# Decode attention over two head blocks: the load order of the last units, finer pieces of the last K and V, and the place of two unit sums on the matmul engine

## The chip, the cores and the metric

The kernel runs on one core of one Trainium2 chip. The metric is the device time of one execution in microseconds (us). Lower is better. The kernel before takes 1973.36 us, the median of 3 runs (1972.6 to 1973.85).

## What is computed

The reference is one decode step of attention for two independent blocks, A and B, of the same shape, whose outputs stand side by side. Each block has a batch of 2, one query token, 32 heads, 8192 cached positions and a head width of 192, all in bf16:

```python
q = (x @ wq).reshape(B, Sq, Hq, Dh).transpose(0, 2, 1, 3)       # x: 2 x 1 x 640
scores = einsum("bhqd,bhkd->bhqk", q, k_cache) * (Dh ** -0.5)   # 8192 scores a head
p = softmax(scores, axis=-1)
o = einsum("bhqk,bhkd->bhqd", p, v_cache)
out = o.transpose(0, 2, 1, 3).reshape(B, Sq, Hq * Dh) @ wo      # 2 x 1 x 640
```

Every element of both caches is used once. The caches are nearly all of the 836.77 MB that the kernel reads.

## The kernel before

**Units.** The work is cut into 64 units, numbered 0 to 63. Unit u is one pair of heads (hp = u // 2, 32 pairs over both blocks) for one batch element (b = u % 2). Its K is one transfer of 6144 KB, and its V another. Both go to one of three buffers `kv` of 128 partitions, in which each of the two heads has 64 partitions, and each partition has T = 128 positions of 192 values.

**The steps of a unit.** Times are those of the profile.

- VectorE (DVE) multiplies K by the broadcast query, in four chunks of 32 positions: `dve_mul`, L226, 3.35 us each, into two `prod` buffers in turn. A chunk needs the sums of the chunk two before it to be done, since they read the same buffer.
- TensorE (PE) adds up a chunk's products: `pe_sum`, L309, 12 matmuls against the identity. For most units the four chunks stand in a loop of instructions (`pe_sums`); for units 62 and 63 they stand one by one.
- DVE finishes the sums (`dve_red`, L229) and takes the maximum (`dve_max`, L235). GpSimd (POOL) brings the maximum to all partitions (L218). ScalarE (ACT) makes the exponentials (`act_nb` L251, `act_exp` L259), and POOL and DVE the sum's reciprocal (L221, L243).
- PE multiplies by V: `pe_pv`, L329, 64 matmuls for one unit. It is called the V product below.
- For each pair of heads, ACT takes the result out of PSUM (`act_f1`, L268), PE turns it (`pe_f3`, L339, 12 matmuls for a pair, or 6 for one batch element), ACT scales it (`act_f4`, L275), and PE multiplies it by `wo` (`pe_f5`, L352, 6 matmuls).

**The order of each engine** is written out by hand. Each step is put in a table at a slot (about the unit) with an order number inside the slot, and the engine runs its table in that order. What an engine is told to wait for blocks all that stands behind it. In most slots u, PE runs the sums of unit u, the `f3` of a finished pair and then the V product of unit u - 1. At the end the order of PE is another one: the sums of units 62 and 63 are in slot 61 (L376, order 1.9), so PE runs the sums of 61, 62 and 63, and only then the V products of 60, 61 and 62. The V product of 63 is cut in pieces that follow its loads, with the `f3` of batch element 0 after the first. The last four `f5` (pairs 28 to 31) close the program.

**Loads.** All K, V and `wo` loads are issued by SyncE (SP), in one queue and in the order of the list `loads` (L138 to L146). Load number i goes to buffer i % 3, and SP waits before it until load i - 3 is used up: `done()`, L431, which is the last `dve_mul` for a K and the last V product matmul for a V. The list alternates: K of unit u, then V of unit u - 1. At the end, lines 144 to 146 take K 62 and K 63 out and put them ahead of V 60. So the last loads are K 61, K 62, K 63, V 60, V 61, V 62, V 63. `VSPLIT` cuts V 62 in two halves and V 63 in pieces of 1/2, 1/4, 1/8, 1/16 and 1/16, and each piece has a semaphore of its own. `KSPLIT` is empty. The four parts of the last `wo` follow V 63 (L448), and each of the last four `f5` waits for its part.

Of the kernel before, what the change touches and what calls it, by code (L numbers as in the profile page):

```python
# [58 lines left out]
def build_kernel(nc, blocks, out):  # L59
# [4 lines left out]
    T = Sk // 64  # L64
# [8 lines left out]
    PW = HW // 2  # L73
    UW = PW * B
    NW = NBLK * Hn // HW
    NP = NBLK * Hn // 2
    NU = NP * B
    LASTP = NP - 1
    LASTU = NU - 1
# [8 lines left out]
    with ExitStack() as es:  # L88
# [35 lines left out]
        S_sp = _Stream("sp", sem("s_sp"), reg)  # L124
# [6 lines left out]
        xsem = [sem(f"xsem{k}") for k in range(NBLK)]  # L131
        osem = [sem(f"osem{k}") for k in range(NBLK)]

        KSPLIT = {}
        VSPLIT = {LASTU - 1: [0, T // 2, T],
                  LASTU: [0, T // 2, 3 * T // 4, 7 * T // 8, 15 * T // 16, T]}

        loads = []  # L138
        for u in range(NU):
# [1 line left out]
            if u >= 1:  # L141
                loads.append(("v", u - 1))
        loads.append(("v", LASTU))
        for u in (LASTU - 1, LASTU):
            loads.remove(("k", u))
            loads.insert(loads.index(("v", LASTU - 3)), ("k", u))  # L146
        buf = {}
        bcount = [0] * NBUF
        for i, (kind, u) in enumerate(loads):
# [29 lines left out]
        def back(name, u, c, n):  # L179
            i = u * NCH + c - n  # L180
            return (name, i // NCH, i % NCH) if i >= 0 else None
# [124 lines left out]
        def pe_sum(c):  # L306
            def fn(eng):
                for j in range(NJ):
                    ins = eng.matmul(scps[c % 2][:], ident[:], prod[c % 2][:, :, j * DG:(j + 1) * DG],  # L309
                                     start=(j == 0), stop=(j == NJ - 1))  # L310
                return ins
            return fn
# [21 lines left out]
        def pe_f3(bs):  # L334
            def fn(eng):
                for b in bs:
                    for i in range(3):
                        for s in range(2):
                            ins = eng.matmul(oTps[64 * s:64 * s + 64, 2 * i + b:2 * i + b + 1],  # L339
                                             o_sb[:, b, :].rearrange("p (r i) -> p i r", i=3)[:, i, :],  # L340
                                             sel[:, s:s + 1], start=True, stop=True)
                return ins
            return fn

        def pe_f5(hp):
            first = (hp % PPB == 0)
            last = (hp % PPB == PPB - 1)

            def fn(eng):
                for i in range(3):  # L350
                    for half in range(2):
                        ins = eng.matmul(outps[0:4, 0:NH2], oTz[:, hp % NZ, i, 2 - 2 * half:6 - 2 * half],  # L352
                                         wo_t[:, hp % PW, i, half * NH2:(half + 1) * NH2],
                                         start=(first and i == 0 and half == 0),
                                         stop=(last and i == 2 and half == 1))
                return ins
            return fn
# [4 lines left out]
        pe_tab = [[] for _ in range(NSLOT)]  # L362
        pool_tab = [[] for _ in range(NSLOT)]

        def put(tab, slot, order, fn, waits, sig):
            tab[slot].append((order, len(tab[slot]), fn, waits, sig))

        for u in range(NU):
            hp = u // B
            for c in range(NCH):  # L370
                kw = [("k", u, c)] if u in KSPLIT else [("k", u)]
                put(dve_tab, u, 2 + 2 * c, dve_mul(u, c), kw + [("a0", u), back("s", u, c, 2)], ("m", u, c))
                put(dve_tab, u, 2 + 2 * min(c + 1, NCH - 1) + 1, dve_red(u, c),
                    [("s", u, c), key("mx", u - 2), key("exp", u - 2)], ("r", u, c))
                if u >= LASTU - 1:
                    put(pe_tab, LASTU - 2, 1.9, pe_sum(c), [("m", u, c), back("r", u, c, 2), ("init",)], ("s", u, c))  # L376
            if u < LASTU - 1:
                put(pe_tab, u, 0, pe_sums(u), [back("r", u, 1, 2), ("init",)], [("s", u, c) for c in range(NCH)])
            put(dve_tab, u, 12, dve_max(u), [("r", u, NCH - 1), key("ar", u - 2), ("init",)], ("mx", u))
            put(pool_tab, u, 0, pool_ar(u), [("mx", u), key("nb", u - 2)], ("ar", u))  # L380
            put(pool_tab, u, 1, pool_ls(u), [("exp", u), key("f2", u - 2)], ("ls", u))
            put(dve_tab, u + 1, 14, dve_f2(u), [("ls", u), key("f4", hp - 2)], ("f2", u))
            put(act_tab, u, 0, act_nb(u), [("ar", u), key("exp", u - 2)], ("nb", u))
            put(act_tab, u, 1, act_exp(u), [("nb", u), key("pv", u - 2), key("ls", u - 2), ("init",)], ("exp", u))
            w0 = [("exp", u), key("f1", hp - 2), ("init",)]
            cuts = VSPLIT.get(u)
            if cuts is None:
                put(pe_tab, u + 1, 2, pe_pv(u, 0, TJ), w0 + [("v", u)], ("pv", u))
            else:
                for i, (t0, t1) in enumerate(zip(cuts[:-1], cuts[1:])):  # L390
                    put(pe_tab, u + 1, 2 + 0.01 * i, pe_pv(u, t0 // 2, t1 // 2), (w0 if i == 0 else []) + [("v", u, i)],
                        ("pv", u) if t1 == T else None)
            sl = UW * (u // UW - 1) + 5 + (u % UW) // 2 if u >= UW else (u - 1) // 2
            order = (-1 if u < 2 else 4)
            put(pe_tab, max(sl, 0), order, pe_q(u), [("wq", u // UW), ("xbc", hp // PPB)], ("pq", u))
            put(act_tab, max(sl, 0), order, act_a0(u), [("pq", u), back("m", u - NQ, NCH - 1, 0)], ("a0", u))

        for hp in range(NP):
            u0, u1 = 2 * hp, 2 * hp + 1
            w1 = [key("f3", hp - 1), ("init",)]  # L400
            w3 = [("sel",), ("init",)]
            w4 = [("f2", u0), key("f5", hp - NZ), ("init",)]
            if hp < LASTP:
                put(act_tab, u1 + 1, 2, act_f1(hp, 0, 2), [("pv", u0), ("pv", u1)] + w1, ("f1", hp))
                put(pe_tab, u1 + 2, 1.5 if hp < LASTP - 1 else 2.5, pe_f3((0, 1)), [("f1", hp)] + w3, ("f3", hp))
                put(act_tab, u1 + 2, 3, act_f4(hp, (0, 1)), [("f3", hp), ("f2", u1)] + w4, ("f4", hp))
            else:
                put(act_tab, u1 + 1, 2, act_f1(hp, 0, 1), [("pv", u0)] + w1, ("f1a", hp))
                put(pe_tab, u1 + 1, 2.005, pe_f3((0,)), [("f1a", hp)] + w3, ("f3a", hp))
                put(act_tab, u1 + 1, 3, act_f4(hp, (0,)), [("f3a", hp)] + w4, ("f4a", hp))  # L410
                put(act_tab, u1 + 2, 2, act_f1(hp, 1, 2), [("pv", u1), ("f3a", hp)], ("f1", hp))
                put(pe_tab, u1 + 2, 1.5, pe_f3((1,)), [("f1", hp)] + w3, ("f3", hp))
                put(act_tab, u1 + 2, 3, act_f4(hp, (1,)), [("f3", hp), ("f2", u1), ("f4a", hp)], ("f4", hp))
            w = hp // PW
            w5 = [("f4", hp), key("f5", hp - 1)]
            if hp % PPB == 0 and hp > 0:
                w5.append(("oev", hp // PPB - 1))
            if w < NW - 1:
                sl = UW * w + 11
                put(pe_tab, sl, 1.6, pe_f5(hp), w5 + [("wo", w)], ("f5", hp))  # L420
            else:
                sl = NU + 1
                put(pe_tab, sl, 1.4 if hp % PW == 0 else 1.6, pe_f5(hp), w5 + [("wol", hp % PW)], ("f5", hp))
            if hp % PPB == PPB - 1:
                blk = hp // PPB
                put(act_tab, sl, 5, act_out(blk), [("f5", hp)], ("oev", blk))
                put(act_tab, sl, 6, out_dma(blk, 0), [("oev", blk)], None)
                if blk < NBLK - 1:
                    put(act_tab, sl, 7, out_dma(blk, 1), [("oev", blk)], None)
# [6 lines left out]

        S_sp.add(sp_wq(0))
        for i, (kind, u) in enumerate(loads):
            for n, fn in enumerate(sp_kv(kind, u)):
                S_sp.add(fn, waits=[done(i - NBUF)] if n == 0 else [])  # L440
            if kind == "k":
                if u % UW == 5 and u // UW + 1 < NW:
                    w = u // UW
                    S_sp.add(sp_wq(w + 1), waits=[("pq", UW * w + UW - 1), key("f5", PW * w - 1)])
                if u >= UW + 3 and u % UW == 3:
                    w = u // UW - 1
                    S_sp.add(sp_wo(w), waits=[("pq", UW * (w + 1) + UW - 1)])
        for q in range(PW):  # L448
            S_sp.add(sp_wo(NW - 1, q), waits=[("f5", PW * (NW - 1) - 1)])
        S_sp.add(out_dma(NBLK - 1, 1), waits=[("oev", NBLK - 1)])  # L450

        S_pool.add(lambda eng: eng.memset(ident[:], 1.0), sig=("id0",))
# [108 lines left out]
```

## Time and profile before

| what | value |
|---|---|
| median of the runs shown | 1973.36 us (1972.6 to 1973.85, 3 runs) |
| the profiled execution: device time | 1973.09 us |
| the profiled execution: span on the core | 1971.4 us |
| granted clock of TensorE, mean | 0.956 |
| PE busy | 1571.2 us (80%) |
| DVE busy | 1067.4 us (54%) |
| ACT, POOL busy | 196.5 us, 60.2 us |
| read from HBM | 836.77 MB, 424 GB/s over the span |
| rate from 100 to 1700 us | 431 GB/s, DMA busy share 1.00 |

The span is 1.69 us shorter than the device time of the same execution. Times inside the program are given from the start of the span. The time between a load's issue and its landing is read from the table of DMA issues, asked for a window around the issue; a landing is the issue plus that time. "x64" in a row is the number of instructions merged in it, and a bracket at its end is the idle time before it and what ended it.

### The profile page before, as it was taken

What the parts mean: (1) busy time and instruction counts of PE and PEld (TensorE: products, weight loads), DVE (VectorE), ACT (ScalarE), POOL (GpSimd) and SP (SyncE); (2) the same over time, 40 slices, a digit from 0 to 9 for tenths busy, and PEclk for the clock granted to TensorE, in tenths of its full rate; (3) what the DMA queues carried; (4) which work ended last, traced back from release to release, by engine and by line L of the source; (5) the groups of instructions that cost most, each with busy time, mean ns of one, the idle gap of its engine ahead of it and who ended that gap; (6) DMA issues with size and microseconds to landing.
All of it is one profiled execution on the core that took longest, in us unless ns stands there. A gap on an engine that the chain in (4) does not pass through costs nothing.

```text
span 1971.4 us, 19404 instructions
## 1 busy us (share of the span) xinstructions
PE 1571.2 (80%) x8448; PEld 772.2 (39%) x8448; DVE 1067.4 (54%) x772; ACT 196.5 (10%) x647; POOL 60.2 (3%) x145
## 2 busy tenths in 40 slices
PE   3887877878778688787887878877788777888769
PEld 1443434434334344343443434433344333443325
DVE  5664565545654556545556455464554654645570
ACT  0110110001100011000110101100011001110001
POOL 1000000000000000000000000000000000000000
PEclk9998999989989899998999989999999999999989
DMA  9999999999999999999999999999999999999986
GB/s 403 431 431 434 431 431 434 430 426 434 431 432 427 435 434 430 429 426 435 433 433 427 431 434 431 431 427 434 430 430 433 432 427 433 435 433 425 434 374 272
DMA packets 29334, 837.81 MB, mean 425 GB/s; under 512 B 3016, under 2 KB 3024, under 8 KB 12624
## 3 DMA queue, kind: packets, MB, share of 16 engines
q1 hardware_dynamic: 28676, 836.77, 98.9%
q8 instruction: 55, 0.90, 0.2%
q10 hardware_dynamic: 588, 0.01, 0.0%
q14 instruction: 15, 0.12, 0.0%
HBM read 836.77 MB, written 0.01 MB: 424 GB/s over the span
## 4 chain that ended last, share of the span: by engine, by line
DMA 50%; PE 28%; DVE 19%; issue 2%; ACT 0%; SPq 0%
DMA kv<-in_A_k_cache_dram 24%; DMA kv<-in_B_k_cache_dram 24%; PE ops L329 18%; DVE prod L226 17%; PE scps L309 9%; DVE sc L229 2%; DMA kv<-in_B_v_cache_dram 2%; PE outps L352 0%; PE qps L339 0%; PE qps L301 0%; DVE mp L235 0%; SPq L185 0%; ACT qbc L284 0%; DVE rcT L243 0%; ACT out_sb L289 0%
## 5 line engine op out<-in xcount | busy, mean ns | idle before, releaser
L226 DVE TENSOR_TENSOR prod<-kv,qbc 128x6144 bf16<-128x6144 bf16 x256 | 852.7, 3351 | 637.7 <-DMA kv<-in_B_k_cache_dram 321.0
L309 PE MATMUL scps<-prod,ident 128*128 128x512 bf16 x3072 | 769.5, 407 | 360.3 <-DVE prod L226 360.3
L329 PE MATMUL ops<-kv,pb 128*34 128x384 bf16 x4096 | 676.6, 326 | 1.3 <-DMA kv<-in_B_v_cache_dram 1.1
L309 PEld LDWEIGHTS scps<-prod,ident 128*128 128x128 bf16 x3072 | 300.2, 103 | 822.2 <-DVE prod L226 459.1
L329 PEld LDWEIGHTS ops<-kv,pb 128*34 128x34 bf16 x4096 | 395.6, 98 | 274.1 <-issue 15.5
L229 DVE TENSOR_REDUCE sc<-scps 128x32 f32<-128x512 f32 x256 | 175.8, 687 | 201.8 <-PE scps L309 201.8
L251 ACT ACTIVATE nb<-mg 64x1 f32<-64x1 f32 x128 | 25.7, 201 | 1313.6 <-POOL mg L218 1312.8
L301 PE MATMUL qps<-wbuf,xbc 128*128 128x384 bf16 x320 | 64.7, 334 | 35.0 <-ACT qbc L284 24.5
L259 ACT ACTIVATE pb<-sc,nb 64x128 bf16<-64x128 f32 x128 | 81.7, 638 | 31.9 <-PE ops L329 28.8
L218 POOL PARTITION_ALL_REDUCE mg<-mp x64 | 26.0, 406 | 1716.5 <-DVE mp L235 1716.5
L284 ACT ACTIVATE qbc<-qps 64x192 bf16<-64x192 f32 x128 | 41.6, 325 | 181.5 <-PE qps L301 180.3
L301 PEld LDWEIGHTS qps<-wbuf,xbc 128*128 128x128 bf16 x320 | 26.5, 99 | 70.3 <-ACT qbc L284 36.8
L268 ACT ACTIVATE o_sb<-ops 2x384 f32<-2x384 f32 (+1 forms) x66 | 31.1, 471 | 223.9 <-PE ops L329 223.5
L339 PEld LDWEIGHTS qps<-sel,o_sb 34*64 34x64 f32 x768 | 36.3, 171 | 13.6 <-issue 13.3
L339 PE MATMUL qps<-sel,o_sb 34*64 34x1 f32 x768 | 39.1, 225 | 0.0
L259 ACT ACTIVATION_READ_ACCUMULATOR pb<-sc,nb 64x1 f32 x128 | 38.6, 301 | 0.0
L235 DVE TENSOR_REDUCE mp<-sc 64x1 f32<-64x128 f32 x128 | 35.9, 280 | 3.1
L243 DVE RECIPROCAL rcT<-lall 64x1 f32<-64x1 f32 x128 | 20.1, 157 | 25.4 <-POOL lall L221 22.5
L221 POOL PARTITION_ALL_REDUCE lall<-rs x64 | 27.9, 436 | 157.5 <-ACT pb L259 157.5
L352 PE MATMUL outps<-wbuf,oTz 128*4 128x320 bf16 x192 | 31.3, 299 | 1.4
L352 PEld LDWEIGHTS outps<-wbuf,oTz 128*4 128x4 bf16 x192 | 13.7, 84 | 16.3 <-PE outps L352 8.9
L275 ACT ACTIVATE oTz<-qps,rcT 128x3 bf16<-128x3 f32 x64 | 13.7, 268 | 15.5 <-PE qps L339 14.7
(19 smaller groups left out, 15.8 us busy)
## 6 DMA issues: line engine op xcount, KB each, us to landing
kv<-in_A_k_cache_dram SPq DMA_DIRECT2D x32, 6144.0 KB, 29.6
kv<-in_A_v_cache_dram SPq DMA_DIRECT2D x32, 6144.0 KB, 29.4
kv<-in_B_k_cache_dram SPq DMA_DIRECT2D x32, 6144.0 KB, 30.3
kv<-in_B_v_cache_dram SPq DMA_DIRECT2D x30, 6144.0 KB, 30.4
kv<-in_B_v_cache_dram SPq DMA_DIRECT2D x3, 3072.0 KB, 12.0
wbuf<-in_A_wq_dram SPq DMA_DIRECT2D x4, 1920.0 KB, 33.1
wbuf<-in_A_wo_dram SPq DMA_DIRECT2D x4, 1920.0 KB, 32.5
wbuf<-in_B_wq_dram SPq DMA_DIRECT2D x4, 1920.0 KB, 33.5
```

The source lines that it names most:

```text
L221: return lambda eng: eng.partition_all_reduce(lall[u % 2][:], rs[u % 2][:], 128, bass.bass_isa.ReduceOp.add)
L226: return lambda eng: eng.tensor_tensor(prod[c % 2][:], t[:, c * TC:(c + 1) * TC, :], q, ALU.mult)
L229: return lambda eng: eng.tensor_reduce(sc[u % 2][:, c * TC:(c + 1) * TC], scps[c % 2][:], AXL.X, ALU.add)
L235: ins = eng.tensor_reduce(mp[u % 2][r, s:s + 1], sc[u % 2][r, :], AXL.X, ALU.max)
L259: ins = eng.activation(pb[u % 2][r, :, s::32], sc[u % 2][r, :].rearrange("p (j a) -> p j a", a=2), ACTF.Exp, bias=nb[u % 2][r, :], scale=s ...
L268: ins = eng.activation(o_sb[r, b0:b1, :], ops[hp % 2][r, b0:b1, a * Dh:(a + 1) * Dh], ACTF.Identity)
L284: ins = eng.activation(qbc[u % NQ][r, :], qps[r, s * Dh:(s + 1) * Dh], ACTF.Identity)
L301: ins = eng.matmul(qps[:, 0:QW], xbc[b][:, c, :], wq_t[:, c, off:off + QW], start=(c == 0), stop=(c == DC - 1))
L309: ins = eng.matmul(scps[c % 2][:], ident[:], prod[c % 2][:, :, j * DG:(j + 1) * DG], start=(j == 0), stop=(j == NJ - 1))
L329: ins = eng.matmul(ops[(u // B) % 2][0:MP, u % B, 0:QW], pb[u % 2][:, j, :], vv[:, j, :], start=(j == 0), stop=(j == TJ - 1))
L339: ins = eng.matmul(oTps[64 * s:64 * s + 64, 2 * i + b:2 * i + b + 1], o_sb[:, b, :].rearrange("p (r i) -> p i r", i=3)[:, i, :], sel[:, s: ...
L352: ins = eng.matmul(outps[0:4, 0:NH2], oTz[:, hp % NZ, i, 2 - 2 * half:6 - 2 * half], wo_t[:, hp % PW, i, half * NH2:(half + 1) * NH2], sta ...
```

## The change

- The special order of the last K loads is removed. K and V alternate to the end: K 61, V 60, K 62, V 61, K 63, V 62, V 63.
- K 62 and K 63 are loaded in four quarters each, one for each chunk of the multiply, with a semaphore for each. V 61 is now in halves as V 62 is, and V 63 is in seven pieces: 1/4, 1/4, 1/8, 1/8, 1/8, 1/16 and 1/16.
- On PE the sums of 62 and 63 stand in their own slots. The order becomes: sums 61, `f3` of pair 29, V product 60, sums 62, V product 61, sums 63, `f3` of pair 30, V product 62, V product 63 in seven pieces.
- The `f5` of pair 28 is moved ahead of the last three pieces of the V product of 63, and its part of `wo` ahead of V 63 in the queue of SP.

No arithmetic is added or removed. From K 62 on, the K and V loads go from 10 transfers to 19.

```diff
-        KSPLIT = {}
-        VSPLIT = {LASTU - 1: [0, T // 2, T],
-                  LASTU: [0, T // 2, 3 * T // 4, 7 * T // 8, 15 * T // 16, T]}
+        QUART = [0, T // 4, T // 2, 3 * T // 4, T]
+        HALF = [0, T // 2, T]
+        KSPLIT = {LASTU - 1: QUART, LASTU: QUART}
+        VSPLIT = {LASTU - 2: HALF, LASTU - 1: HALF,
+                  LASTU: [0, T // 4, T // 2, 5 * T // 8, 3 * T // 4, 7 * T // 8, 15 * T // 16, T]}
...
         loads.append(("v", LASTU))
-        for u in (LASTU - 1, LASTU):
-            loads.remove(("k", u))
-            loads.insert(loads.index(("v", LASTU - 3)), ("k", u))
...
-                if u >= LASTU - 1:
-                    put(pe_tab, LASTU - 2, 1.9, pe_sum(c), [("m", u, c), back("r", u, c, 2), ("init",)], ("s", u, c))
-            if u < LASTU - 1:
+                if u in KSPLIT:
+                    put(pe_tab, u, 0.1 * c, pe_sum(c), [("m", u, c), back("r", u, c, 2), ("init",)], ("s", u, c))
+            if u not in KSPLIT:
                 put(pe_tab, u, 0, pe_sums(u), [back("r", u, 1, 2), ("init",)], [("s", u, c) for c in range(NCH)])
...
-                put(pe_tab, u1 + 2, 1.5 if hp < LASTP - 1 else 2.5, pe_f3((0, 1)), [("f1", hp)] + w3, ("f3", hp))
+                put(pe_tab, u1 + 2, 1.5, pe_f3((0, 1)), [("f1", hp)] + w3, ("f3", hp))
...
-                put(pe_tab, sl, 1.4 if hp % PW == 0 else 1.6, pe_f5(hp), w5 + [("wol", hp % PW)], ("f5", hp))
+                put(pe_tab, NU if hp % PW == 0 else sl, 2.035 if hp % PW == 0 else 1.6, pe_f5(hp), w5 + [("wol", hp % PW)], ("f5", hp))
...
         for i, (kind, u) in enumerate(loads):
+            if i == len(loads) - 1:
+                S_sp.add(sp_wo(NW - 1, 0), waits=[("f5", PW * (NW - 1) - 1)])
             for n, fn in enumerate(sp_kv(kind, u)):
...
-        for q in range(PW):
-            S_sp.add(sp_wo(NW - 1, q), waits=[("f5", PW * (NW - 1) - 1)])
+        for q in range(1, PW):
+            S_sp.add(sp_wo(NW - 1, q))
```

## The prediction

> **What bounds the kernel now.** I read the page first, then the rates by window, then the chain of waits, then the timelines of PE and DVE at the end. Up to about 1890 us the loads set the pace: the DMA share is 1.00 and 431 GB/s flow from 100 to 1700 us. No order of work can shorten that part, and the change touches nothing in it. The windows at the end differ (columns: window, length, busy time of PE, PEld, DVE, ACT and POOL with instruction counts, PE clock, DMA share, GB/s):
>
> ```profile
> 1890.00:1895.00 5.00, 3.54 (x17) 1.48 (x16) 5.00 (x4) 0.00 (x0) 0.00 (x0) 1.00 0.84 364
> 1895.00:1900.00 5.00, 3.90 (x19) 1.58 (x17) 3.21 (x2) 0.00 (x0) 0.00 (x0) 1.00 0.78 295
> ...
> 1915.00:1920.00 5.00, 3.90 (x19) 1.60 (x18) 3.67 (x2) 0.00 (x0) 0.00 (x0) 1.00 0.52 167
> ```
>
> The loads run short, because SP holds V 61 and V 62 back until the multiplies of K 62 and K 63 are done. But that is not what ends last. The chain of waits (start, length, what) is:
>
> ```profile
> 1902.16 3.37 DVE prod L226
> 1905.53 0.04 issue
> 1905.57 4.65 PE scps L309 x12
> ...
> 1918.13 2.76 PE scps L309 x12
> 1920.89 31.31 PE ops L329 x192
> 1952.20 1.15 PE qps L339 x24
> 1953.35 5.30 PE ops L329 x32
> 1958.65 0.62 PE qps L339 x12
> 1959.27 5.31 PE ops L329 x32
> ```
>
> From 1861 to 1921 us DVE and PE take turns over the sums of 61, 62 and 63. Then PE does four V products one after another with no gap. The last piece of V 63 is issued at 1933.22 and takes 17.7 us, so it lands at 1950.9, before PE takes up V 63 at all (1953.28). Hence PE's order bounds the end. The timeline of PE says what it loses:
>
> ```profile
> 1879.91 1.22 PE L339 MATMUL qps<-sel,o_sb 34*64 34x1 f32 x24
> 1885.12 7.21 PE L309 MATMUL scps<-prod,ident 128*128 128x512 bf16 x24 [4.00 <-DVE prod L226]
> ...
> 1905.57 7.23 PE L309 MATMUL scps<-prod,ident 128*128 128x512 bf16 x24 [5.15 <-DVE prod L226]
> ```
>
> PE waits 4 and 5 us for DVE at the start of each unit, while V products that it could run (V 60 landed at 1905.1, issue 1877.18 plus 27.9) stand behind in its queue.
>
> **The change part by part.** The comparison starts at 1879.91, where PE begins the f3 of pair 29 in both orders; nothing before it moves, except that V 60 takes K 62's place in the queue.
>
> *PE's order.* Before, from 1879.91 to the start of V 63 at 1953.28: 73.37 us. After, the pieces are:
>
> - f3 of two pairs: 1.15 each (the x24 row of the chain).
> - V products 60, 61, 62: 31.31 / 3 = 10.44 each.
> - the sums of 62 and of 63. The rows to price these are unit 60's:
>
> ```profile
> 1838.38 0.68 DVE L229 TENSOR_REDUCE sc<-scps 128x32 f32<-128x512 f32 x1
> 1838.98 3.35 DVE L226 TENSOR_TENSOR prod<-kv,qbc 128x6144 bf16<-128x6144 bf16 x1
> 1842.24 0.68 DVE L229 TENSOR_REDUCE sc<-scps 128x32 f32<-128x512 f32 x1
> 1842.84 3.35 DVE L226 TENSOR_TENSOR prod<-kv,qbc 128x6144 bf16<-128x6144 bf16 x1
> ...
> 1848.94 10.57 PE L329 MATMUL ops<-kv,pb 128*34 128x384 bf16 x64
> ```
>
> The first two multiplies need no sums, so in the new order they are done while PE is still in the V product. The sums of chunk 0 then start with no wait: 2.76 + 0.04 to the first reduction. From there the rows give 1848.94 - 1838.38 = 10.56 to the next V product (chunks 2 and 3 take turns between DVE and PE). Together 13.36 a unit, against 20.4 before (1902.16 - 1881.71).
>
> Sum: 2 x 1.15 + 3 x 10.44 + 2 x 13.36 = 60.34 us, **13.03 us less**.
>
> *The last pieces.* V 63's 64 matmuls and the f3 between them are the same work. The f5 of pair 28 (0.90, 1964.51 to 1965.41) lay beside ACT's copy f1 before. Now it stands ahead of the last pieces, and the f1 after them is uncovered: **0.90 us more**. More pieces add only waits. From the last V matmul to the end nothing changes (1964.51 to 1971.4).
>
> *Are the data there?* This is the only cover that could be missing. PE would reach V 60 at 1881.1, the sums of 62 at 1891.5, V 61 at 1904.9, the sums of 63 at 1915.3, V 62 at 1929.8, and the seven pieces of V 63 at 1940.3, 1943.5, 1946.1, 1947.4, 1949.6, 1950.9 and 1951.6. The loads are taken in queue order from the landing of the load after K 61, at 1875.8 (K 62 before, issue 1846.22 plus 29.6; V 60 now, of the same 6144 KB, which is 6.29 MB). Spacings between landings before: 7.31 for 3072 KB (1936.1 to 1943.4), then 3.71 for 1536 KB, 1.90 for 768, 0.98 for 384, and 1.2 to 1.4 for 480 KB of wo. With four quarters 14.84 and two halves 14.62, K 62 lands by 1890.6, V 61 by 1905.3, K 63 by 1920.1, V 62 by 1934.7, wo part 0 at 1935.9, and V 63's pieces at 1939.6, 1943.3, 1945.2, 1947.1, 1949.0, 1950.0 and 1951.0; the other wo parts by 1954.8, used last at 1955.7. So every piece is there, but only **0.1 to 0.9 us early**. The second half of V 61 (1905.3) is not needed until 1910. K 62's first two quarters land by 1883.2, K 63's by 1912.7; their multiplies are done by 1888.4 and 1916.1, and the sums of chunk 1 of 63 start at 1918.
>
> *Does SP issue in time?* A load must be issued before the one ahead of it lands. V 61 waits as now (1877.2). K 63 waits for V product 60: 1891.5, while V 61 flies until 1905. V 62 waits for the last multiply of 62, at 1902.2, while K 63 flies until 1920. V 63 waits for V product 61: 1915.3, while V 62 flies until 1934.7. Behind each waiting instruction stand only later loads and the output. The issues (0.33 to 0.47 us, once 1.30) lie beside transfers. Moving wo part 0 past V 63 delays V 63 by 1.2 us, counted above.
>
> *Unseen costs.* A K in quarters is not in the trace. Its nearest row is 1536 KB of V at 3.71 us, 0.08 over a quarter of 14.53. The other end is the wo row at 1.39 where 1.2 is usual: 0.2 a piece, 3 us over 15 pieces. Below nothing there is no reason. I take 0.08. Sums one by one instead of in the loop: both forms stand in the trace with 2.76, so nothing.
>
> Another price is stated by the Trainium skill, "DMA: Bandwidth & Descriptors", Anatomy of one DMA: about 2.0 us fixed for each DMA, and its rules ask for 1 MiB or more each. That speaks against this change: nine more transfers would be 18 us, landing the last wo near 1973 and ending the span near 1976, slower than before. But the trace has 384 KB pieces landing 0.98 us apart, where the rule would give 2.9, so with loads queued behind each other the fixed part is hidden here.
>
> **Sum.** -13.03 + 0.90 = -12.13. The profiled execution took 1973.09 us (span 1971.4): 1961.0, span 1959.3. It lies 0.27 below the median of the runs. With 0.1 for the tightest pieces I say **1961.1**.
>
> **Rivals.**
>
> - *The loads become the bound.* For: margins of 0.1 to 0.9 us, and one half of V 62 took 8.3 us instead of 7.3. Against: landings 14.5 to 14.9 us apart while a load is always queued. From 1919.7 to 1956.0, 14.55 MB took 36.3 us, 401 GB/s. At that rate the 33.4 MB after 1875.8 end at 1959.1 instead of 1954.8, 3.4 us past the margin: 1962 to 1964.5.
> - *The quarters do not land in turn,* so DVE begins K 63 at 1920.1 only: whole-K rows give 17.1 us to the end of its sums (1831.83 to 1848.94), 1937.2 instead of 1928.7. 1969.5. Against: V 63's pieces landed in turn.
> - *PE at a lower clock, slower than before.* PE's first sums after 5.15 us of idling took 4.65 instead of 2.76, a factor 1.7. If the short waits of the new order (1.1 to 1.5 us between chunks) hold the clock down between 1881 and 1952, each us of PE work costs 0.7 more. From 23 us of such work on, of 41.8 in the four V products, 16 us are lost and the end is past 1977. Against: after waits of 1.1 to 2.2 us rows show 2.76.
>
> **How the numbers follow.** Forecast 0.70, loads 0.21, quarters 0.04, clock 0.05. Under 0.2% (3.9 us) a measurement of this kernel can hardly tell from none. Faster: 0.70 + 0.21 = 0.91. Same: 0.04 (1969.5). Slower: 0.05. The range runs from 1959.4 (no extra load cost, and a run as far below the median as 1972.6 is) to 1964.6 (the loads' end) and leaves out the last two.
>
> **What would show it.** Right: V product 60 starting near 1881 and the sums of 62 directly after it; 13 to 14 us from V product to V product; V 63 starting near 1940; no window under 400 GB/s until about 1945. Wrong: waits of PE on V 63's pieces above 1 us (loads), sums of 63 starting near 1924 (quarters), or x12 rows of 4.6 us after 1891 (clock).

## The result, and the profile after

The changed kernel takes **1961.47 us** (median of 6 runs, 1960.68 to 1962.36), the kernel before 1973.61 beside it (6 runs, 1972.6 to 1975.52). The ratio is 0.9938, with a 95% interval of 0.9925 to 0.9951: 12 us, or 0.6%, faster. The span of the profiled execution is 1959.1 us; 1959.3 was worked out.

The chain of waits of the changed kernel, from the V product of unit 60 on (start, length, what). Its lines are numbered one less than before:

```profile
1880.86 10.51 PE ops L328 x64
1891.36 2.71 PE scps L308 x12
...
1901.98 2.76 PE scps L308 x12
1904.74 10.51 PE ops L328 x64
1915.25 2.71 PE scps L308 x12
...
1925.86 2.76 PE scps L308 x12
1928.62 1.15 PE qps L338 x24
1929.77 13.11 PE ops L328 x80
1942.88 0.62 PE qps L338 x12
1943.50 5.30 PE ops L328 x32
1948.80 0.91 PE outps L351 x6
1949.71 2.72 PE ops L328 x16
```

The reader is to see that sums and V products now alternate, that the first sums of a unit start the moment a V product ends, and that no row names a load after 1880.86. Before, three V products stood in one row of 31.31 us behind the sums. The sums of 62 begin at 1891.36 and the next V product at 1904.74: 13.4 us a unit, where 20.4 was needed before.

The same windows of the loads, and the lowest one ahead of 1945:

```profile
1890.00:1895.00 5.00, 5.00 (x27) 2.29 (x25) 0.90 (x2) 0.00 (x0) 0.00 (x0) 1.00 0.98 415
1895.00:1900.00 5.00, 3.54 (x17) 1.46 (x16) 5.00 (x3) 0.00 (x0) 0.00 (x0) 1.00 0.97 415
...
1915.00:1920.00 5.00, 5.00 (x25) 2.23 (x24) 2.83 (x3) 0.96 (x2) 0.00 (x0) 1.00 0.99 423
...
1940.00:1945.00 5.00, 5.00 (x40) 3.11 (x39) 0.00 (x0) 0.91 (x3) 0.00 (x0) 1.00 0.86 352
```

The pauses at 1890 to 1900 and 1915 to 1920 (364, 295 and 167 GB/s before) are gone. The loads still end only 2 us earlier: the last part of wo lands at 1954.0, against 1956.0 before (issue plus time to landing). The gain is PE's.

### The profile page after: what moved, and what is told of

Read it like the earlier page. It is cut to its first block, busy times and chain, and to the rows that moved or that the text cites. A ratio compares the mean times of both kernels' runs of the same rounds, so it can differ in the third digit from the quotient of the medians.

```text
span 1959.1 us, 19412 instructions
## 1 busy us (share of the span) xinstructions
PE 1574.1 (80%) x8448; PEld 772.9 (39%) x8448; DVE 1067.5 (54%) x772; ACT 196.5 (10%) x647; POOL 60.0 (3%) x145
## 4 chain that ended last, share of the span: by engine, by line
DMA 49%; PE 29%; DVE 19%; issue 3%; ACT 0%; SPq 0%
DMA kv<-in_A_k_cache_dram 24%; DMA kv<-in_B_k_cache_dram 23%; PE ops L328 18%; DVE prod L225 17%; PE scps L308 9%; DVE sc L228 2%; DMA kv<-in_B_v_cache_dram 2%; PE qps L338 1%; PE outps L351 1%; PE qps L300 0%; SPq L184 0%; ACT qbc L283 0%; ACT out_sb L288 0%; ACT o_sb L267 0%; DVE mp L234 0%
```

## The experiments

Two readings had to be told apart. **Theory:** the order of PE and DVE sets the end, the quarters of K let DVE work beside a V product, and the loads land less than 1 us ahead of their use. **Rivals:** the gain is that of loads that no longer pause; PE's order gives it by itself; or PE sets the end alone, and the loads are far ahead.

**Both K whole**

```diff
-        KSPLIT = {LASTU - 1: QUART, LASTU: QUART}
+        KSPLIT = {}
-                if u in KSPLIT:
+                if u >= LASTU - 1:
-            if u not in KSPLIT:
+            if u < LASTU - 1:
```

> The changed kernel, but K 62 and K 63 are each one transfer again; all else stays. Theory (the order of PE and DVE sets the end, the quarters let the first two multiplies run beside the V product): DVE can begin K 63 only when all of it has landed, near 1919.8 in the changed kernel's trace; unit 60's rows give 17.1 us from there to the next step of PE, 1936.9 instead of 1928.6, so the span is 8.3 us longer than the changed kernel's 1959.1: 1967.4, time about 1969.5. Rival (the gain comes from loads that no longer pause; a K in one piece moves the same bytes): no difference, span 1959 to 1960.

Measured: 1970.66 us, 0.9987 of the kernel before (0.9978 to 0.9997), span 1969.3. K 63 landed at 1919.4, and the loads flowed as in the changed kernel (last wo part at 1953.6). So flowing loads alone are not the gain: without the quarters, 10.2 of the 12.3 us between the spans are gone, 1.9 more than the 8.3 expected. The profiled run is one of the longer ones of this kernel (spans 1967.8 to 1969.8); by the medians 9.2 us are gone. The rows of PE (start, length, last the idle time before and what ended it) say where:

```profile
1893.81 7.04 PE L308 MATMUL scps<-prod,ident 128*128 128x512 bf16 x24 [3.03 <-DVE prod L225]
...
1922.83 8.18 PE L308 MATMUL scps<-prod,ident 128*128 128x512 bf16 x24 [3.37 <-DVE prod L225]
```

In the changed kernel these 24 matmuls take 5.35 us with no idle time ahead of them. Here the granted clock is 0.59 in the window 1893.8 to 1897.5 and 0.50 from 1922.8 to 1928. The step from K 63 to the end of its sums took 19.3 us (1919.41 to 1938.73) instead of the 17.1 of unit 60, whose rows were at full clock.

**K 62 alone whole**

```diff
-        KSPLIT = {LASTU - 1: QUART, LASTU: QUART}
+        KSPLIT = {LASTU: QUART}
```

and the two conditions as above.

> The changed kernel, but K 62 alone is one transfer; K 63 stays in quarters. Theory: the first multiply of 62 ends at 1890.4 + 3.4 = 1893.8 instead of 1884.8, and the V product of 60 covers until 1891.3, so the sums end 17.1 us after 1890.4, at 1907.5 instead of 1904.7: 2.8 us longer, span 1961.9, time about 1964. Rival (the loads set the end, and pieces only add a cost per transfer): same or up to 0.3 us shorter.

Measured: 1963.73 us, 0.9955 (0.9939 to 0.9972), span 1961.6: 2.5 us longer than the changed kernel, as the theory has it. The V product of 61 starts at 1907.12, 17.1 us after K 62's landing at 1890.0. K 62 landed only 1.4 us before the V product of 60 ended, so little of its multiplies was hidden, and PE idled for 1.97 us ahead of the sums. K 63 comes later against PE: whole, it landed at 1919.4, 4.1 us after the V product of 61 ends in the changed kernel (1915.25). So the larger part of the 10.2 us should be K 63's, but a run with K 63 alone whole was not made.

**The order alone**

```diff
-        KSPLIT = {LASTU - 1: QUART, LASTU: QUART}
-        VSPLIT = {LASTU - 2: HALF, LASTU - 1: HALF,
-                  LASTU: [0, T // 4, T // 2, 5 * T // 8, 3 * T // 4, 7 * T // 8, 15 * T // 16, T]}
+        KSPLIT = {}
+        VSPLIT = {LASTU - 1: [0, T // 2, T],
+                  LASTU: [0, T // 2, 3 * T // 4, 7 * T // 8, 15 * T // 16, T]}
```

with the two conditions as above and the f5 of pair 28 and its part of wo back at their old places.

> Only the alternating load order and the new place of the sums of 62 and 63 on PE; K whole, V pieces, the f5 of pair 28 and the parts of wo as in the kernel before. Theory: K 63's landing near 1919.8 sets the end as in the run with both K whole (8.3 us over the changed kernel), and the f5 beside the copy gives 0.9 back: span 1966.5, time about 1968.5, so 5 of the 12 us are the order's and 7 come with the pieces. Rival (loads that no longer pause): all of the gain stays, 1959 to 1960.

Measured: 1969.38 us, 0.9984 (0.9974 to 0.9994), span 1967.4. So 4.0 us are the order's (3.2 by the medians), and 8.3 us come with the pieces and the new place of the f5, which by itself costs 0.9. The 0.9 beyond the expected span is again the clock: the first sums of 63 (1922.68, after 4.81 us of idling) took 7.04 instead of 5.35, while K 63 landed 0.6 us earlier than expected.

**PE's order alone, on the kernel before**

```diff
-                    put(pe_tab, LASTU - 2, 1.9, pe_sum(c), ...)
+                    put(pe_tab, u, 0.1 * c, pe_sum(c), ...)
-                put(pe_tab, u1 + 2, 1.5 if hp < LASTP - 1 else 2.5, pe_f3((0, 1)), ...)
+                put(pe_tab, u1 + 2, 1.5, pe_f3((0, 1)), ...)
```

> The kernel before, with the new place of the sums of 62 and 63 and of the f3 of pair 30 on PE only; the old load order and pieces. Theory (PE's order pays only if V 60 comes ahead of K 62): V 60 lands at 1905.1, PE stands until then; the last multiply of 62 ends near 1928, SP holds V 61 until then, it lands near 1945, and so on with V 62: the last V piece lands near 2000, span about 2007, time about 2009, 35 us slower than before. Rival (PE's order by itself gives the 13 us): span near 1958.

Measured: 2016.13 us, 1.0217 (1.0200 to 1.0234), span 2014.8: 43 us slower. The rows of PE:

```profile
1904.24 13.37 PE L329 MATMUL ops<-kv,pb 128*34 128x384 bf16 x64 [25.27 <-DMA kv<-in_B_v_cache_dram]
...
1945.38 13.26 PE L329 MATMUL ops<-kv,pb 128*34 128x384 bf16 x64 [14.40 <-DMA kv<-in_B_v_cache_dram]
...
1979.58 13.24 PE L329 MATMUL ops<-kv,pb 128*34 128x384 bf16 x64 [6.41 <-DMA kv<-in_B_v_cache_dram]
1995.00 7.04 PE L329 MATMUL ops<-kv,pb 128*34 128x384 bf16 x32 [2.17 <-DMA kv<-in_B_v_cache_dram]
```

Each V product waits for its load, and each load for a multiply that waits for the V product before it. Between 1910 and 1920 the loads move 2 GB/s. Of the 8 us beyond the expectation, the clock, which the expectation left out, gives about 4: the V product of 61 took 13.3 us instead of 10.5, so the last piece of V 63 landed at 2002.5 instead of near 2000, and the first half of V 63 took 7.04 instead of 5.38. The rest was reckoned wrongly: the expectation let the span end 7 us after that landing, but the first half of V 63 landed only at 1994.9, and PE needed 12.9 us from 1995.0 for all of V 63. The span ended 12.3 us after the last landing. The opposite half, the new load order with PE's old order, was not tried: K 63 would need the buffer of V 60, whose product would stand on PE behind the sums of K 63, and nothing would go on.

**The old pieces of V**

```diff
-        VSPLIT = {LASTU - 2: HALF, LASTU - 1: HALF,
-                  LASTU: [0, T // 4, T // 2, 5 * T // 8, 3 * T // 4, 7 * T // 8, 15 * T // 16, T]}
+        VSPLIT = {LASTU - 1: [0, T // 2, T],
+                  LASTU: [0, T // 2, 3 * T // 4, 7 * T // 8, 15 * T // 16, T]}
```

> The changed kernel with the V pieces of the kernel before: V 61 whole, V 63 in 1/2, 1/4, 1/8, 1/16, 1/16. Theory: PE reaches V 63 at 1940.2, and its first half lands only near 1943.0, so PE waits 2.8 us there; V 61 whole costs 0.4 us (lands 1905.1, wanted 1904.7). All of it goes to the end, less at most 0.3 of waits that move: span 1961.9 to 1962.3, time near 1964. Rival (pieces cost something per transfer, the loads set the end): 0.3 us shorter.

Measured: 1964.59 us, 0.9960 (0.9945 to 0.9976), span 1962.1: 3.0 us longer. PE waited 0.60 us for V 61 and 2.32 for the first half of V 63:

```profile
1943.15 5.36 PE L328 MATMUL ops<-kv,pb 128*34 128x384 bf16 x32 [2.32 <-DMA kv<-in_B_v_cache_dram]
```

**Half of three V products left out**

```diff
-                for j in range(j0, j1):
+                st = 2 if LASTU - 3 <= u < LASTU else 1
+                for j in range(j0, j1, st):
...
-                                     start=(j == 0), stop=(j == TJ - 1))
+                                     start=(j == 0), stop=(j == TJ - st))
```

> The changed kernel with every second matmul left out of the V products of units 60, 61 and 62 (half the sum over positions is missing there); all loads and waits stay. It takes 15.7 us of work from PE's chain. Theory (the loads stand 0.1 to 0.9 us behind PE's chain): PE then waits for the second half of V 62 near 1934.4 and for V 63's pieces, and the span shortens by 0.5 us only, to about 1958.6. Rival (PE alone sets the end, the loads are far ahead): span near 1944 to 1950.

Measured: 1960.47 us, 0.9939 (0.9924 to 0.9955), span 1958.5. PE lost 15.7 us of work and the span 0.6. The rows name the loads now:

```profile
1934.22 4.07 PE L329 MATMUL ops<-kv,pb 128*34 128x384 bf16 x16 [3.48 <-DMA kv<-in_B_v_cache_dram]
1939.19 2.76 PE L329 MATMUL ops<-kv,pb 128*34 128x384 bf16 x16 [0.90 <-DMA kv<-in_B_v_cache_dram]
...
1942.80 5.38 PE L329 MATMUL ops<-kv,pb 128*34 128x384 bf16 x32 [0.23 <-DMA kv<-in_B_v_cache_dram]
```

From 1942.80 on PE does what it does in the changed kernel, only 0.63 us earlier, and what it waited for there is the second quarter of V 63. In the changed kernel that quarter landed at 1943.01 and was taken up at 1943.43. So PE's chain and the loads stand less than 1 us apart: both set the end, and a shortening of PE's work ahead of V 63 is worth no more than that.

**The f5 of pair 28 back, then K 61 in quarters too, then V 62 in quarters too**

```diff
-                put(pe_tab, NU if hp % PW == 0 else sl, 2.035 if hp % PW == 0 else 1.6, pe_f5(hp), ...)
+                put(pe_tab, sl, 1.4 if hp % PW == 0 else 1.6, pe_f5(hp), ...)
-            if i == len(loads) - 1:
-                S_sp.add(sp_wo(NW - 1, 0), waits=[("f5", PW * (NW - 1) - 1)])
...
-        for q in range(1, PW):
-            S_sp.add(sp_wo(NW - 1, q))
+        for q in range(PW):
+            S_sp.add(sp_wo(NW - 1, q), waits=[("f5", PW * (NW - 1) - 1)])
```

> The changed kernel with the f5 of pair 28 and its part of wo at their old places, behind V 63. Theory: the f5 again lies beside the copy f1, which takes 0.9 us off PE's chain, and V 63's pieces land 1.2 us earlier: span 1958.2, 0.9 shorter than the changed kernel. Rival (the early f5 filled a wait for loads and was free, and wo is now late): same or up to 1 us longer.

The second version adds `LASTU - 2: QUART` to `KSPLIT`:

> A version meant to beat both: K 61 in quarters as well, and the f5 of pair 28 and its part of wo at their old places. Theory: the sums of 61 end 7 us earlier, but PE then meets the loads (second half of V 62 near 1934.4, wo parts until 1954): span 1957.6, 1.5 shorter than the changed kernel, time near 1959.7. Rival (PE's chain alone): 7.9 us shorter, span near 1951. Rival (cost per transfer): 0.3 us longer than the run with the f5 moved back alone.

The third is the second with `LASTU - 1` in `VSPLIT` changed from `HALF` to `QUART`. It ran beside the changed kernel and the first version once more, on one chip:

> The version with K 61 in quarters and the f5 of pair 28 at its old place, with V 62 in quarters too. In the run before it PE waited for the second half of V 62 until 1934.5 and then had 23.3 us of work left. Theory (the loads are now the bound): with quarters only 16 of 64 matmuls stay behind 1934.5, PE then follows V 63's pieces, the last of which lands at 1949.4; plus 0.65 and 6.85 that is a span of 1957.0, and the last part of wo (1954.1, plus its f5, the copy and the store, 3.2) gives 1957.3: 0.5 us shorter. Rival (each of these is inside the scatter of the runs): no difference from 1957.8.

> The changed kernel as it is, beside the versions on one chip: span 1958.6 to 1960.4 as in its six runs, time near 1961.5. Theory: 1.5 to 2 us longer than the two other kernels of this call. Rival (the versions are not faster, the chip was another one): the same time as they.

> The changed kernel with the f5 of pair 28 and its part of wo at their old places, again, since in its first profile the sums of 61 ran 1.3 us earlier by the clock. Theory: 0.9 us shorter than the changed kernel on the same chip, if PE's first sums of 61 take as long in both; rival (the gain was that clock): same.

| kernel | time, us (5 runs each) | to the kernel before (95%) | span |
|---|---|---|---|
| f5 back, first runs | 1959.70 | 0.9935 (0.9922 to 0.9949) | 1958.0 |
| f5 back, K 61 in quarters, first runs | 1959.55 | 0.9935 (0.9922 to 0.9949) | 1957.8 |
| changed kernel, second runs | 1960.56 (1960.26 to 1960.69) | 0.9936 (0.9923 to 0.9950) | 1958.8 |
| f5 back, second runs | 1959.82 (1959.54 to 1960.47) | 0.9934 (0.9921 to 0.9948) | 1957.8 |
| f5 back, K 61 and V 62 in quarters, second runs | 1959.97 (1959.22 to 1960.74) | 0.9933 (0.9919 to 0.9946) | 1957.8 |

*The f5.* In the second runs both kernels start the second half of V 62 nearly together (1934.65 in the changed one, worked out as 1929.43 plus 5.22; 1934.53 with the f5 back). From there the spans are 24.15 and 23.27 us long: 0.88 apart, the 0.90 that the prediction put on this move, and no row of PE waits for a load in that stretch. The medians are 0.74 apart. That is under 0.04% of the time, and the ranges overlap, so the profiles carry this finding more than the times do. The changed kernel was expected to be 1.5 to 2 us longer than the two versions beside it; it was 0.7 and 0.6 longer. It took 0.9 us less than in its first runs (1961.47), while the version with the f5 back took the same, so more than half of the first distance of 1.8 us was one between runs, not between kernels.

*K 61 in quarters* brings the sums of 61 to an end 6 us earlier than in the changed kernel (1873.84 instead of 1879.64), and the end almost nothing: PE then waits for the second half of V 62 until 1934.55, as it does without that edit (1934.53).

```profile
1934.55 7.97 PE L328 MATMUL ops<-kv,pb 128*34 128x384 bf16 x48 [1.66 <-DMA kv<-in_B_v_cache_dram]
```

The rival of PE's chain alone, a span near 1951, is refuted. *V 62 in quarters* was to give 0.5 and gave none. PE followed V 63's pieces as said, but then waited for the first part of wo:

```profile
1950.99 0.97 PE L351 MATMUL outps<-wbuf,oTz 128*4 128x320 bf16 x6 [0.38 <-DMA wbuf<-in_B_wo_dram]
```

That f5 stands ahead of the last f3, which could have run near 1951.4 (the last V matmul ends at 1950.6, the copy takes 0.8) and starts at 1951.90. All three versions end within 0.2 us of each other, and in each of them PE waits for a load after 1934. So making PE faster ahead of V 62 brings nothing more. Whether the last f3 ahead of that f5 would bring the 0.5 us was not tried.

## Why the prediction was right

Time and sign came out as forecast (1961.1 forecast, 1961.47 measured). That the two lie within 0.4 us is partly luck, as the same kernel took 1960.56 in its second runs. The steps came out too, as the two profiles and the runs show:

- *PE's order, -13.03.* PE was to reach V 60 at 1881.1, the sums of 62 at 1891.5, V 61 at 1904.9, the sums of 63 at 1915.3 and V 62 at 1929.8. It did so at 1880.8, 1891.3, 1904.7, 1915.2 and 1929.7. The f3 of pair 29 began at 1879.64, 0.27 earlier than before, which no term said; from there to V 63, at 1940.2 by the rows, it took 60.5 us where 60.34 was worked out.
- *The f5, +0.90.* Shown by moving it back: 0.88.
- *The loads come in time, 0.1 to 0.9 us early.* V 63's first quarter landed at 1939.3 and its last piece at 1950.5, where 1939.6 and 1951.0 were worked out. No wait of PE on a load is left after 1881. The margin was as thin as said: V 63's second quarter landed 0.4 us ahead of its use, and 15.7 us less work for PE moved the end by 0.6.
- *A quarter of K costs 0.08 over its share.* K 62's quarters landed at 1879.4, 1883.1, 1886.8 and 1890.4, 3.7 apart.
- *The fixed price of a DMA.* With nine more transfers of K and V the last part of wo landed 2 us earlier, and not near 1973; V 63's two 384 KB pieces landed 0.94 and 0.96 us after the piece ahead of each. The page that the prediction names measured its 2.0 us on DMAs that GpSimd issues, while these loads are issued by SP.
- *The quarters land in turn.* Had they not, the run with both K whole shows the price. Said was 8.4 us (1969.5); the medians give 9.2 and the two profiles 10.2, since the clock falls there too.
- *The clock.* After 1891 all sums of the changed kernel took 2.76 us for twelve matmuls and 5.35 for 24. The short waits of 1.1 to 1.5 us did not hold the clock down in either profile of it. That short waits can is shown by another run below.

What was off: the prediction said that no window would be under 400 GB/s until about 1945. Three were: 393 (1860 to 1865), 391 (1870 to 1875) and 352 (1940 to 1945). The first two lie ahead of the changed order of PE, and the landings were in time all the same. In the third, only V 63's later pieces and wo were left. What each load in turn lands at tells more here than the rate of a window.

Two points of the prediction were not tested: loads at 401 GB/s, and a clock held down for the whole end, since nothing in these runs brought either about.

## What to carry to other kernels

Where two engines hand chunks to each other and one of them waits at the start of each round, put work that needs neither between the rounds, and cut the next input so finely that the first handover lies beside that work. Such an order on the engine pays only with the order of the loads that fits it: by itself it was 43 us slower, because buffers came free too late. Then list, for each piece, when it is wanted and when it lands; that list told here both the gain and where it stops.

## What the runs showed of the hardware

The length of an idle stretch does not decide by itself whether PE's clock falls. After 3.54 us of idling (f5 back, first runs) twelve matmuls took the full-clock 2.76 us:

```profile
1864.64 2.76 PE L308 MATMUL scps<-prod,ident 128*128 128x512 bf16 x12 [3.54 <-DVE prod L225]
```

After 3.03 us (both K whole) and 3.02 us (half V products) 24 matmuls took 7.04 instead of 5.35. After 1.97 us (K 62 whole) and 2.19 us (the kernel before, 1835.25) they ran at full clock. Idling of about that length lost the clock too: after 2.57 us (half V products, 1904.85) 16 matmuls took 4.06 instead of 2.77, and after 2.17 us (PE's order alone, 1995.00) 32 took 7.04 instead of 5.38. In the run with V 62 in quarters a wait of 0.83 us behind the small matmuls of an f3 was enough:

```profile
1875.96 12.26 PE L328 MATMUL ops<-kv,pb 128*34 128x384 bf16 x64 [0.83 <-DMA kv<-in_B_v_cache_dram]
```

The granted clock was 1.00 up to 1876.7, 0.50 from there to 1880.1 and 1.00 after it. With 0.73 us at the same place (K 61 in quarters) the 64 matmuls took 10.57. Nothing came of the 1.7 us lost, since PE waited for loads at the end.

The Trainium skill, "TensorE: Matmul & The Clock Gate", Part 1, says that activity is judged in a window of about 3.4 us that runs freely. These runs agree so far that idling of like length went both ways, between 2.17 and 3.54 us, and that the clock stayed down for 3.4 us from 1876.7 on. They also show that PE need not idle for the length of such a window to lose the clock. So the full clock at the end of the changed kernel is what its two profiles have, and not a thing that short waits make sure of.

From K 61's landing to the end of its sums it made 17.1 us with the f5 back (first runs), 18.5 in the changed kernel's first profile and 18.9 in its second. The second has the shorter span all the same (1958.8), as K 61 landed 0.65 us earlier there. What makes up the spread of the changed kernel's spans (1958.6 to 1960.4 in six runs) the runs do not show.

SP's issue of one load, 0.33 to 0.47 us as a rule, took 6.35 us for V 63's last piece in the changed kernel and 5.57 for the next one. Neither half of V 62 had landed by then, so 14.5 MB of V 62, V 63 and wo were under way or to come. Nothing waited for SP then; why it took so long stays open.
